# The router's gate on two fp32r parts of y and 32 columns, in place of three bf16 parts and 48

## The chip, the cores and the metric

One NeuronCore of a Trainium2 chip runs the whole program. The metric is the device time of one execution in microseconds. TensorE (PE; its weight loads are shown as PEld), VectorE (DVE), ScalarE (ACT) and GpSimd (POOL) run beside each other; SyncE (SP) issues most DMAs. Instructions of one engine start in the order in which they stand in its queue.

## The reference

Four batches of 2496 rows by 256 go through a spectral layer, and its output y is the input of a mixture of eight experts with the two best per row.

```python
X = np.fft.rfft(x, axis=1)
Yr = Xr @ w_r - Xi @ w_i + b_r            # and Yi; then soft thresholding with 0.01
y = np.fft.irfft(Yr + 1j * Yi, n=2496, axis=1)

logits = y @ w_gate                       # [9984, 8]
noise_scale = np.log1p(np.exp(y @ w_noise))
noisy_logits = logits + noise_scale * noise
top2 = np.argpartition(-noisy_logits, 2, axis=1)[:, :2]
...                                       # softmax over the two: top2_w
for each expert e, for each row that chose it:
    out += top2_w * (np.maximum(y @ w1[e], 0.0) @ w2[e])
```

The change is in the product of y with `w_gate` and `w_noise`, 16 columns together. Which experts a row chooses depends on it, so it is computed to nearly full float32 precision from parts.

## The kernel before

**Spectral stage.** Each batch is worked off in ten steps, c = 0 to 39 over the four batches. A step makes `z` (`mix`, the products with `w_r` and `w_i`), `y` (`s2`), and the first half of the inverse transform `u` (`is2`, sent to a scratch tensor `ud`). All of these multiply float32 values as fp32r parts: a high part, cast by ScalarE, and the rest, subtracted by VectorE. Between two batches stands stage 1 of the next one (`s1`, product `s`, plain float32).

**Last half and gate.** While batch b+1 goes through the spectral stage, batch b is finished in 11 tiles of up to 2 x 117 rows (the last has 2 x 78): `fin` makes the rows `f` and copies them to `yf`, `gate_a` transposes them on PE into `yt` and takes the first part, `gate_b` takes the others, `gate_c` multiplies them by the weights into `lg` and sums the parts with a reduction into `ls`. In these products the piece of y is the stationary operand (117 or 78 columns), the weights are the moving one. `route` then turns `ls` into choices, and `scatter` sends the rows to the region of their expert.

**What sets the order.** The steps of `fin`, gate (G), `route` (R) and `scatter` (S) are queued as closures, and two plans name the slot of the main loop at which each is called: `put` in the main loop for batches 0 to 2, two gate steps in each c, and `expert_plan` for batch 3, whose gate runs inside the first expert blocks. A step j of the gate before runs `gate_c(j-2)`, `gate_b(j-1)` and `gate_a(j)`; there are 13 of them per batch. Inside these limits the framework orders each engine's instructions by its own estimate of when their data are ready; only SP's are kept as written. Buffers of the pools are given in the code by `bufs`.

**Experts.** 40 blocks of 512 rows follow; each has 48 products `p` of 512 columns in the first layer (`blk_L1`, parts `hh` and `hl` behind it) and 64 in the second (`blk_L2`). The first block's first layer begins while the last batch leaves the spectral stage. I call this place the hand-over; there VectorE also works off `route` of batch 2, whose tiles are all called `rt`.

Of the kernel before, what the change touches and what calls it, by code (L numbers as in the profile page):

```python
# [43 lines left out]
def expert_plan(todo):  # L44

    mp = {(i, k): "" for i in range(12) for k in range(12)}

    def put(kind, n, i, k, every):
        if len(every) == 1:
            mp[i, k] += kind * n  # L50
            n = 0
        while n:
            if k in every:
                mp[i, k] += kind
                n -= 1
# [81 lines left out]
def tile_spectral_moe(ctx: ExitStack, tc: tile.TileContext, x, w_r, w_i, b_r, b_i, w_gate, w_noise,  # L137
# [77 lines left out]
    w3 = const.tile([128, 2, 48], BF16, name="w3", tag="w3")  # L215
# [32 lines left out]
    def late_loads():  # L248
        Es = tail.tile([117, 22, 39], F32, name="Es", tag="UT", bufs=4)
        last["es"] = Es  # L250
        nc.sync.dma_start(Es, c_inv)
        nc.sync.dma_start(wgn[:, :, 0:NE], w_gate.rearrange("(c p) d -> p c d", p=128))
        nc.sync.dma_start(wgn[:, :, NE:], w_noise.rearrange("(c p) d -> p c d", p=128))
        rest = wgn
        for k in range(3):
            nc.gpsimd.tensor_copy(w3[:, :, 16 * k:16 * k + 16], rest)
            if k < 2:
                nxt = const.tile([128, 2, 16], F32, name=f"wrest{k}", tag=f"wrest{k}")
                nc.gpsimd.tensor_sub(nxt, rest, w3[:, :, 16 * k:16 * k + 16])
                rest = nxt  # L260
        nc.sync.dma_start(nzt, noise)

    def expand_e(a):
# [143 lines left out]
    def np_(j):  # L407
        return PT if j < 10 else 78

    def gate_a(b, j):  # L410

        P, yf = np_(j), YF[b, j]
        yt = ps.tile([128, 2, 2, 128], F32, name=f"yt{b}_{j}", tag="B", bufs=NBK)
        for i in range(2):
            for dc in range(2):
                nc.tensor.transpose(yt[:, i, dc, :P], yf[:P, i, 128 * dc:128 * dc + 128], ident[:P, :P])  # L416
        y3 = tail.tile([128, 3, 2, 2, PT], BF16, name=f"y3{b}_{j}", tag="y3", bufs=2)
        r1 = tail.tile([128, 2, 2, PT], F32, name=f"r1{b}_{j}", tag="r1", bufs=1)
        YS[b, j] = (y3, r1)
        nc.scalar.copy(y3[:, 0, :, :, :P], yt[:, :, :, :P])  # L420
        nc.vector.tensor_sub(r1[:, :, :, :P], yt[:, :, :, :P], y3[:, 0, :, :, :P])

    def gate_b(b, j):
        P = np_(j)
        y3, r1 = YS[b, j]
        nc.scalar.copy(y3[:, 1, :, :, :P], r1[:, :, :, :P])
        nc.vector.tensor_sub(y3[:, 2, :, :, :P], r1[:, :, :, :P], y3[:, 1, :, :, :P])

    def gate_c(b, j):
        P = np_(j)  # L430
        y3, _ = YS.pop((b, j))
        if j == 0:
            LS[b] = tail.tile([PT, TT, 16], F32, name=f"ls{b}", tag="ls", bufs=1)
            nc.vector.memset(LS[b][:, 20:], 0.0)
        if j % 5 == 0:
            LG[b] = ps.tile([128, 10, 48], F32, name=f"lg{b}_{j}", tag="LG", bufs=1)
        for i in range(2):
            o = LG[b][:P, 2 * (j % 5) + i, :]
            for dc in range(2):
                for k in range(3):  # L440
                    nc.tensor.matmul(o, y3[:, k, i, dc, :P], w3[:, dc, :], start=dc == k == 0, stop=dc == 1 and k == 2)  # L441
        if j % 5 == 4 or j == 10:
            h, n = 10 * (j // 5), 10 if j < 10 else 2
            nc.vector.tensor_reduce(out=LS[b][:P, h:h + n], in_=LG[b][:P, :n].rearrange("p t (k c) -> p t c k", k=3),
                                    axis=AX.X, op=ALU.add)

    RT = {}
# [344 lines left out]

    def queue_gate(b):
        def step(j):
            if j >= 2:
                gate_c(b, j - 2)
            if 1 <= j < 12:
                gate_b(b, j - 1)
            if j < 11:
                gate_a(b, j)  # L800

        for j in range(13):
            todo["G"].append(lambda j=j: step(j))

    def queue_route(b):
# [57 lines left out]
    for b in range(NB - 1):  # L863
# [1 line left out]
        f = c + (2, 3, 4)[b]  # L865
        put("U", 1, f - 2, 0, ev)
        put("F", 11, f, 0, (0, 2, 4, 6, 8))
        p = put("G", 13, f, 3, (1, 3, 5, 7, 9))
# [67 lines left out]
    blk_L1(0, 0)  # L936
    ysplit(b, 8)
    s2(b, 9)
    do("G" * (len(todo["G"]) - 13))
    is2(b, 8)  # L940
    blk_L1(0, 1)
    ysplit(b, 9)
# [109 lines left out]
```

## Time and profile before

| | us |
|---|---|
| median of 3 timed runs (lowest, highest) | 1255.1 (1250.47, 1260.01) |
| the profiled execution, its own time | 1242.59 |
| its span, first to last instruction | 1240.9 |
| PE busy | 1214.5 |
| VectorE busy | 837.9 |
| ScalarE busy | 721.5 |
| POOL busy | 472.5 |

The span is what the trace covers; the execution's own time has 1.7 us around it. Busy times are unions of records. PE's records are pipelined: each shows its own latency, so a group's busy time is not its share of PE, and the pace of short matmuls is read from the distances between their starts. The gate of batches 0 to 2 runs from 99 to 317 us, that of batch 3 up to 437 us.

### The profile page before, as it was taken

How to read it: one execution, taken by the hardware profiler on the slowest of the kernel's cores; microseconds unless marked ns; L12 is line 12 of the kernel's file. 1: busy time of each engine (PE TensorE's matmuls, PEld its weight loads, DVE VectorE, ACT ScalarE, POOL GpSimd, SP SyncE). 2: the span in 40 equal slices, each digit the busy share in tenths (PEclk: the TensorE clock that was granted, in tenths of full speed). 3: DMA queues.
4: the chain of work that ended last, by engine and by line, in shares of the span. 5: the costliest groups of instructions: out<-in, count | busy, mean ns of one | idle time of the engine just before them, and what ended most of it. 6: DMA issues, size and time to landing. Idle time of an engine off the chain costs nothing.

```text
span 1240.9 us, 18977 instructions
## 1 busy us (share of the span) xinstructions
PE 1214.5 (98%) x6596; PEld 1030.0 (83%) x6596; DVE 837.9 (68%) x1709; ACT 721.5 (58%) x1367; POOL 472.5 (38%) x374
## 2 busy tenths in 40 slices
PE   7999999999899999999999999999999999999996
PEld 6888888888688888888888888888888888888885
DVE  4867887788866697566665666656566665666652
ACT  3656677778666676565555545555455554555542
POOL 3000035464345677877323232232322323233232
PEclk9999999999999999999999999999999999999998
DMA  6646645265758769996866656666565766657641
GB/s 173 184 146 215 220 125 185 92 210 135 234 120 195 178 157 248 251 248 166 179 132 149 158 140 146 124 152 154 145 149 118 151 154 146 153 118 147 152 98 24
DMA packets 224693, 197.68 MB, mean 159 GB/s; under 512 B 116967, under 2 KB 203901, under 8 KB 224590
## 3 DMA queue, kind: packets, MB, share of 16 engines
q1 hardware_dynamic: 190206, 153.18, 45.9%
q0 software_dynamic: 34384, 43.21, 18.7%
q8 instruction: 54, 0.88, 0.3%
q14 instruction: 49, 0.40, 0.1%
HBM read 107.46 MB, written 67.90 MB: 141 GB/s over the span
## 4 chain that ended last, share of the span: by engine, by line
PE 94%; DVE 2%; DMA 1%; ACT 1%; issue 0%; POOL 0%; SPq 0%; POOLq 0%; ACTq 0%; DVEq 0%
PE p L756 36%; PE p L739 34%; PE z L321 9%; PE y L334 4%; PE f L401 3%; PE u L365 2%; PE lg L441 2%; PE yt L416 1%; DMA wf<-w_i 1%; PE s L291 1%; DMA x<-x 0%; DVE hl L743 0%; ACT L474 0%; DVE rt L489 0%; DVE rt L493 0%
## 5 line engine op out<-in xcount | busy, mean ns | idle before, releaser
L762 POOL DMA_INDIRECT out<-ot,si x160 | 271.3, 1696 | 474.1 <-DVE f L683 344.5
L756 PE MATMUL p<-w2p,hh 128*128 128x512 f32 x1280 | 444.5, 395 | 0.1
L756 PE MATMUL p<-w2p,hl 128*128 128x256 f32 x1280 | 332.4, 280 | 0.7 <-DVE hl L743 0.7
L557 POOL DMA_INDIRECT xs_d<-yx,rt x176 | 190.4, 1082 | 271.8 <-ACT yx L552 210.5
L743 DVE SCALAR_TENSOR_TENSOR hl<-p,hh 128x512 fp32r<-128x512 f32 x320 | 220.1, 688 | 101.7 <-ACT hh L742 100.7
L742 ACT ACTIVATE hh<-p 128x512 fp32r<-128x512 f32 x320 | 191.6, 599 | 134.0 <-PE p L739 133.7
L756 PEld LDWEIGHTS p<-w2p,hh 128*128 128x128 f32 x1280 | 232.4, 188 | 44.1 <-DVE w2p L718 0.4
L739 PE MATMUL p<-xh,w1h 128*128 128x512 f32 x640 | 251.8, 393 | 3.8 <-DVE hl L743 3.8
L756 PEld LDWEIGHTS p<-w2p,hl 128*128 128x128 f32 x1280 | 241.0, 188 | 14.6 <-DVE hl L743 1.3
L739 PE MATMUL p<-xl,w1h 128*128 128x512 f32 x640 | 250.0, 391 | 0.0
L739 PE MATMUL p<-xh,w1l 128*128 128x512 f32 x640 | 249.6, 390 | 0.0
L760 ACT ACTIVATE o<-p,wt 128x256 f32<-128x256 f32 x160 | 75.9, 474 | 243.5 <-PE p L756 243.2
L761 DVE SCALAR_TENSOR_TENSOR ot<-p,wt,o 128x256 f32<-128x256 f32 x160 | 77.1, 482 | 187.3 <-ACT o L760 187.3
L739 PEld LDWEIGHTS p<-xh,w1h 128*128 128x128 f32 x640 | 120.5, 188 | 28.3 <-DVE hl L743 4.7
L739 PEld LDWEIGHTS p<-xh,w1l 128*128 128x128 f32 x640 | 120.6, 188 | 25.3
L739 PEld LDWEIGHTS p<-xl,w1h 128*128 128x128 f32 x640 | 120.6, 188 | 24.9
L718 DVE TENSOR_TENSOR w1l<-w1r,w1h 128x512 fp32r<-128x512 f32 x160 | 108.7, 685 | 15.6 <-ACT w1h L715 15.5
L715 ACT CAST w1h<-w1r 128x512 fp32r<-128x512 f32 x160 | 97.7, 618 | 17.9 <-PE p L739 17.9
L718 DVE TENSOR_TENSOR w2p<-w2r,w2p 128x512 fp32r<-128x512 f32 x160 | 103.8, 687 | 2.2 <-ACT w2p L715 1.2
L715 ACT CAST w2p<-w2r 128x512 fp32r<-128x512 f32 x160 | 91.0, 620 | 0.0
L321 PE MATMUL z<-wh,th 128*128 128x512 f32 x160 | 66.1, 413 | 2.0 <-ACT th L306 2.0
L324 DVE TENSOR_TENSOR zl<-z,zh 128x512 fp32r<-128x512 f32 x80 | 54.8, 687 | 17.4 <-ACT zh L323 16.6
(153 smaller groups left out, 1423.0 us busy)
## 6 DMA issues: line engine op xcount, KB each, us to landing
w1r<-w SPq DMA_DIRECT2D x40, 1024.0 KB
w2r<-w SPq DMA_DIRECT2D x40, 1024.0 KB
out<-zero SPq DMA_DIRECT2D x16, 656.0 KB
x<-x SPq DMA_DIRECT2D x20, 468.0 KB
UT<-ud SPq DMA_DIRECT2D x60, 156.0 KB
ud<-us SPq DMA_DIRECT2D x36, 256.0 KB
xs_d<-zero SPq DMA_DIRECT2D x9, 528.0 KB
xs_d<-yx,rt POOLq DMA_INDIRECT x176, 4.7
```

Source lines behind the costliest of these rows:

```text
L321: nc.tensor.matmul(z, t[:, dc, 128 * h:128 * h + 128], ww[:, dc, :], start=k == 0, stop=k == 5)
L324: nc.vector.tensor_sub(zl[:, h], z, zh[:, h].bitcast(F32))
L557: st = nc.gpsimd.indirect_dma_start(out=xs_d, out_offset=bass.IndirectOffsetOnAxis(ap=ix[:P, 2 * j + n, k:k + 1], axis=0), in_=yx[:P, n, : ...
L715: cp = nc.scalar.copy(h, r)
L718: nc.vector.tensor_sub(l, r, h.bitcast(F32))
L739: nc.tensor.matmul(p, a[:, dc, 128 * f:128 * f + 128], b[:, dc], start=k == 0, stop=k == 5)
L742: last["act"] = nc.scalar.activation(hh, p, AF.Relu).ins
L743: last["dve"] = nc.vector.scalar_tensor_tensor(out=hl, in0=p, scalar=0.0, in1=hh.bitcast(F32), op0=ALU.max, op1=ALU.subtract).ins
L756: nc.tensor.matmul(o, a[:, sl], b, start=f == n == 0, stop=f == 7 and n == 1)
L760: nc.scalar.activation(o1, p[:, 1], AF.Copy, scale=wt)
L761: nc.vector.scalar_tensor_tensor(out=ot, in0=p[:, 0], scalar=wt, in1=o1, op0=ALU.mult, op1=ALU.add)
L762: st = nc.gpsimd.indirect_dma_start(out=out, out_offset=bass.IndirectOffsetOnAxis(ap=si[:, m:m + 1], axis=0), in_=ot, in_offset=None, comp ...
```

## The change

`gate_a` now casts the transposed tile to an fp32r part `gh` and subtracts it from the tile into a second fp32r part `gl`. `gate_b` and its two operations are gone. The weights are two fp32r parts side by side, 32 columns, `w2g`. `gate_c` makes four products for each of the two halves of a tile (two parts by two chunks of 128 of the 256 columns of y), eight per tile in place of twelve; the reduction adds two groups of 16 columns in place of three. A step j of the gate runs `gate_c(j-1)` and `gate_a(j)`, 12 steps per batch, so routing is called one gate slot earlier.

```diff
-    p = put("G", 13, 1, 1, (1, 4, 7, 10))
+    p = put("G", 12, 1, 1, (1, 4, 7, 10))
...
-        rest = wgn
-        for k in range(3):
-            nc.gpsimd.tensor_copy(w3[:, :, 16 * k:16 * k + 16], rest)
-            if k < 2:
-                nxt = const.tile([128, 2, 16], F32, name=f"wrest{k}", tag=f"wrest{k}")
-                nc.gpsimd.tensor_sub(nxt, rest, w3[:, :, 16 * k:16 * k + 16])
-                rest = nxt
+        nc.gpsimd.tensor_copy(w2g[:, :, :16], wgn)
+        nc.gpsimd.tensor_sub(w2g[:, :, 16:], wgn, w2g[:, :, :16].bitcast(F32))
...
-        y3 = tail.tile([128, 3, 2, 2, PT], BF16, name=f"y3{b}_{j}", tag="y3", bufs=2)
-        r1 = tail.tile([128, 2, 2, PT], F32, name=f"r1{b}_{j}", tag="r1", bufs=1)
-        YS[b, j] = (y3, r1)
-        nc.scalar.copy(y3[:, 0, :, :, :P], yt[:, :, :, :P])
-        nc.vector.tensor_sub(r1[:, :, :, :P], yt[:, :, :, :P], y3[:, 0, :, :, :P])
-
-    def gate_b(b, j):
-        P = np_(j)
-        y3, r1 = YS[b, j]
-        nc.scalar.copy(y3[:, 1, :, :, :P], r1[:, :, :, :P])
-        nc.vector.tensor_sub(y3[:, 2, :, :, :P], r1[:, :, :, :P], y3[:, 1, :, :, :P])
+        gh, gl = YS[b, j] = [tail.tile([128, 2, 2, PT], F32R, name=f"g{n}{b}_{j}", tag=f"g{n}") for n in "hl"]
+        nc.scalar.copy(gh[:, :, :, :P], yt[:, :, :, :P])
+        nc.vector.tensor_sub(gl[:, :, :, :P], yt[:, :, :, :P], gh[:, :, :, :P].bitcast(F32))
...
-            LG[b] = ps.tile([128, 10, 48], F32, name=f"lg{b}_{j}", tag="LG", bufs=1)
+            LG[b] = ps.tile([128, 10, 32], F32, name=f"lg{b}_{j}", tag="LG", bufs=1)
         for i in range(2):
-            o = LG[b][:P, 2 * (j % 5) + i, :]
-            for dc in range(2):
-                for k in range(3):
-                    nc.tensor.matmul(o, y3[:, k, i, dc, :P], w3[:, dc, :], start=dc == k == 0, stop=dc == 1 and k == 2)
+            for n in range(4):
+                nc.tensor.matmul(LG[b][:P, 2 * (j % 5) + i, :], g2[n // 2][:, i, n % 2, :P], w2g[:, n % 2, :],
+                                 start=n == 0, stop=n == 3)
...
         def step(j):
-            if j >= 2:
-                gate_c(b, j - 2)
             if 1 <= j < 12:
-                gate_b(b, j - 1)
+                gate_c(b, j - 1)
             if j < 11:
                 gate_a(b, j)
```

The other two lines with 13 (the plan of batches 0 to 2, and the call of what is left before the hand-over) become 12 as well.

On PE, at the first tile of batch 0, the order was this (a matmul with bf16 operands has its load as a row of its own; `w` is the gate's weights):

```order
L416 MATMUL yt_0_960<-ident,yf_0_912 128x117 x4
L334 MATMUL y_2_1014<-zh_2_897,FG 128x512
L321 MATMUL z_4_0_1072<-wh,th_4_999 128x512
L321 MATMUL z_4_0_1072<-wl,th_4_999 128x512
L441 LDWEIGHTS y_0_965
L441 MATMUL lg_0_1045<-w_116,y_0_965 117x48
L321 MATMUL z_4_0_1072<-wh,tl_4_1000 128x512
L321 MATMUL z_4_0_1072<-wh,th_4_999 128x512
L321 MATMUL z_4_0_1072<-wl,th_4_999 128x512
L321 MATMUL z_4_0_1072<-wh,tl_4_1000 128x512
L401 MATMUL f_2_986<-UT_1_834,E 117x256 x2
L416 MATMUL yt_1_1005<-ident,yf_1_942 128x117 x4
```

It is now this:

```order
L411 MATMUL yt_0_955<-ident,yf_0_907 128x117 x4
L329 MATMUL y_2_1018<-zh_2_892,FG 128x512
L316 MATMUL z_4_0_1067<-wh,th_4_994 128x512
L316 MATMUL z_4_0_1067<-wl,th_4_994 128x512
L426 MATMUL lg_0_1000<-w2g,gh_0_960 117x32 x2
L316 MATMUL z_4_0_1067<-wh,tl_4_995 128x512
L316 MATMUL z_4_0_1067<-wh,th_4_994 128x512
L316 MATMUL z_4_0_1067<-wl,th_4_994 128x512
L316 MATMUL z_4_0_1067<-wh,tl_4_995 128x512
L396 MATMUL f_2_981<-UT_1_829,E 117x256 x2
L426 MATMUL lg_0_1000<-w2g,gl_0_961 117x32 x2
L426 MATMUL lg_0_1000<-w2g,gh_0_960 117x32 x2
```

All eight products of the first tile now stand ahead of the second tile's transposes, where one of twelve did.

On PE at the hand-over, the last gate tile of batch 2 (`lg_10`) stood among the first expert block's products:

```order
L365 MATMUL u_8_3841<-yh_8_3790,FG 128x512
L365 MATMUL u_8_3841<-yl_8_3791,FG 128x512
L365 MATMUL u_8_3841<-yh_8_3790,FG 128x512
L739 MATMUL p_1_3848<-xh_3773,w1h_3287 128x512
L739 MATMUL p_1_3848<-xl_3774,w1h_3287 128x512
L739 MATMUL p_1_3848<-xh_3773,w1l_3288 128x512
L739 MATMUL p_1_3848<-xh_3773,w1h_3287 128x512
L441 LDWEIGHTS y_10_3740
L441 MATMUL lg_10_3827<-w_116,y_10_3740 78x48
```

Now:

```order
L426 MATMUL lg_10_3628<-w2g,gh_10_3556 78x32 x2
L426 MATMUL lg_10_3628<-w2g,gl_10_3557 78x32 x2
L426 MATMUL lg_10_3628<-w2g,gh_10_3556 78x32 x2
L426 MATMUL lg_10_3628<-w2g,gl_10_3557 78x32 x2
L360 MATMUL u_8_3638<-yh_8_3606,FG 128x512
L360 MATMUL u_8_3638<-yl_8_3607,FG 128x512
L360 MATMUL u_8_3638<-yh_8_3606,FG 128x512
L725 MATMUL p_1_3645<-xh_3589,w1h_3150 128x512
```

The tile's products have moved ahead of `u_8` and `p_1`.

On VectorE at the same place, before, from the last tile's reduction on (`hl` is the second part behind the experts' first layer, `c`, `yl` belong to the spectral stage):

```order
L444 TENSOR_REDUCE ls_3261<-lg_10_3827 78x32
L743 SCALAR_TENSOR_TENSOR hl_1_3856<-p_1_3848,hh_1_3855 128x512
L470 SCALAR_TENSOR_TENSOR rt_4_3904<-ls_3261 117x176
L356 TENSOR_TENSOR yl_9_3860<-c_9_3808,yh_9_3859 128x512
L473 TENSOR_SCALAR rt_2_3902<-rt_1_3901 117x176
L477 SCALAR_TENSOR_TENSOR rt_4_3904<-rt_2_3902,rt_1_3901 117x176
L478 TENSOR_TENSOR rt_3_3903<-rt_3_3903,rt_4_3904 117x176
```

Now:

```order
L430 TENSOR_REDUCE ls_3086<-lg_10_3628 78x32
L342 TENSOR_SCALAR c_9_3624<-t_9_3623 128x512
L456 SCALAR_TENSOR_TENSOR rt_4_3701<-ls_3086 117x176
L343 TENSOR_TENSOR c_9_3624<-t_9_3623,c_9_3624 128x512
L459 TENSOR_SCALAR rt_2_3699<-rt_1_3698 117x176
L463 SCALAR_TENSOR_TENSOR rt_4_3701<-rt_2_3699,rt_1_3698 117x176
L351 TENSOR_TENSOR yl_9_3657<-c_9_3624,yh_9_3656 128x512
L729 SCALAR_TENSOR_TENSOR hl_1_3653<-p_1_3645,hh_1_3652 128x512
L464 TENSOR_TENSOR rt_3_3700<-rt_3_3700,rt_4_3701 117x176
```

The reduction and the first of the routing now stand ahead of `c_9`, and `hl_1` has moved behind the routing's first three operations and `yl_9`.

## Rows read from the trace of the kernel before

**Rows 1.** The page, parts 1 and 4: busy times, and the chain that ended last.

```profile
PE 1214.5 (98%) x6596; PEld 1030.0 (83%) x6596; DVE 837.9 (68%) x1709; ACT 721.5 (58%) x1367; POOL 472.5 (38%) x374
...
PE 94%; DVE 2%; DMA 1%; ACT 1%; issue 0%; POOL 0%; SPq 0%; POOLq 0%; ACTq 0%; DVEq 0%
PE p L756 36%; PE p L739 34%; PE z L321 9%; PE y L334 4%; PE f L401 3%; PE u L365 2%; PE lg L441 2%; PE yt L416 1%; DMA wf<-w_i 1%; PE s L291 1%; DMA x<-x 0%; DVE hl L743 0%; ACT L474 0%; DVE rt L489 0%; DVE rt L493 0%
```

**Rows 2.** Busy times by stretch: length, PE, PEld, DVE, ACT, POOL, clock, DMA.

```profile
99.00:145.00 46.00, 46.00 (x326) 38.42 (x326) 36.28 (x63) 30.90 (x57) 0.00 (x0) 1.00 0.69 221
...
310.00:331.00 21.00, 17.22 (x102) 13.92 (x101) 17.19 (x42) 12.67 (x23) 6.32 (x6) 0.92 0.64 190
```

**Rows 3.** Waits of PE: total us, times, longest.

```profile
PE lg L441 <- DVE y L427: 0.4, 1, 0.4
PE yt L416 <- DVE r L421: 0.4, 1, 0.4
```

**Rows 4.** Groups by line and shape: busy us, mean ns, idle before.

```profile
L441 PE MATMUL lg<-w,y 128*117 128x48 bf16 x480 | 33.0, 210 | 0.6 <-DVE y L427 0.4
L427 DVE TENSOR_TENSOR y<-r,y 128x468 bf16<-128x468 f32 x40 | 25.7, 643 | 7.9 <-ACT y L426 7.6
L426 ACT CAST y<-r 128x468 bf16<-128x468 f32 x40 | 23.5, 588 | 13.8 <-DVE r L421 13.8
L441 PE MATMUL lg<-w,y 128*78 128x48 bf16 x48 | 2.6, 194 | 0.0
```

**Rows 5.** Timeline of PE at 107 us: start, us, instruction.

```profile
107.55 0.78 PE L441 MATMUL lg<-w,y 128*117 128x48 bf16 x12
```

**Rows 6.** Timeline of PE at 316 us, the hand-over.

```profile
315.82 0.48 PE L739 MATMUL p<-xl,w1h 128*128 128x512 f32 x1
316.14 0.39 PE L739 MATMUL p<-xh,w1l 128*128 128x512 f32 x1
316.37 0.53 PE L441 MATMUL lg<-w,y 128*78 128x48 bf16 x10
317.94 0.50 PE L739 MATMUL p<-xh,w1h 128*128 128x512 f32 x1 [1.05 <-DVE hl L743]
```

**Rows 7.** Timeline of PE, stage 1 of batches 1 and 2.

```profile
78.76 0.72 PE L291 MATMUL s<-C,x 78*128 78x80 f32 x5
...
158.15 2.82 PE L291 MATMUL s<-C,x 117*128 117x120 f32 x24
```

**Rows 8.** Records by line: min/median/max ns, first and last start, forms.

```profile
L291 PEld LDWEIGHTS s<-C,x x352: 186/192/338, 6.1 to 240.6; 117*128 117x128 f32 x160, 78*128 78x128 f32 x16
L291 PE MATMUL s<-C,x x352: 242/275/537, 6.1 to 240.7; 117*128 117x120 f32 x160, 78*128 78x80 f32 x16
...
L756 PEld LDWEIGHTS p<-w2p,hl x1280: 186/188/208, 331.8 to 1229.3; 128*128 128x128 f32 x183
...
L441 PEld LDWEIGHTS <-y x528: 113/134/136, 100.3 to 436.8; 128*117 128x117 bf16 x160, 128*78 128x78 bf16 x16
...
L416 PEld LDWEIGHTS yt<-ident,yf x176: 137/141/168, 99.0 to 421.7; 117*128 117x128 f32 x160, 78*128 78x128 f32 x16
...
L401 PE MATMUL f<-UT,E x176: 377/378/475, 96.3 to 408.9; 117*117 117x256 f32 x160, 78*78 78x256 f32 x16
```

**Rows 9.** Timeline of PE at 602 us, the experts' second layer.

```profile
601.75 0.28 PE L756 MATMUL p<-w2p,hl 128*128 128x256 f32 x1
601.86 0.39 PE L756 MATMUL p<-w2p,hh 128*128 128x512 f32 x1
```

**Rows 10.** Timeline at the hand-over, VectorE's routing and PE's long wait.

```profile
317.80 0.33 DVE L470 SCALAR_TENSOR_TENSOR rt<-ls 117x176 f32<-117x176 f32 x1
...
325.14 0.17 DVE L501 TENSOR_TENSOR rt<-rt,rt 117x22 f32<-117x22 f32 x1
...
325.97 0.80 PE L739 MATMUL p<-xh,w1h 128*128 128x512 f32 x1 [2.74 <-DVE hl L743]
```

**Rows 11.** Busy times by stretch, right behind that wait.

```profile
326.00:329.00 3.00, 3.00 (x7) 2.44 (x8) 2.31 (x4) 0.07 (x1) 0.00 (x0) 0.50 0.80 227
```

More of the change, by code (lines that the diff above doesn't have):

```diff
@@ L214, in tile_spectral_moe @@
     wgn = const.tile([128, 2, 16], F32, name="wgn", tag="wgn")
-    w3 = const.tile([128, 2, 48], BF16, name="w3", tag="w3")
+    w2g = const.tile([128, 2, 32], F32R, name="w2g", tag="w2g")
     nzt = const.tile([PT, NB * TT, NE], F32, name="nzt", tag="nzt")
@@ L416, in gate_a @@
                 nc.tensor.transpose(yt[:, i, dc, :P], yf[:P, i, 128 * dc:128 * dc + 128], ident[:P, :P])
-        y3 = tail.tile([128, 3, 2, 2, PT], BF16, name=f"y3{b}_{j}", tag="y3", bufs=2)
-        r1 = tail.tile([128, 2, 2, PT], F32, name=f"r1{b}_{j}", tag="r1", bufs=1)
-        YS[b, j] = (y3, r1)
-        nc.scalar.copy(y3[:, 0, :, :, :P], yt[:, :, :, :P])
-        nc.vector.tensor_sub(r1[:, :, :, :P], yt[:, :, :, :P], y3[:, 0, :, :, :P])
-    def gate_b(b, j):
-        P = np_(j)
-        y3, r1 = YS[b, j]
-        nc.scalar.copy(y3[:, 1, :, :, :P], r1[:, :, :, :P])
-        nc.vector.tensor_sub(y3[:, 2, :, :, :P], r1[:, :, :, :P], y3[:, 1, :, :, :P])
+        gh, gl = YS[b, j] = [tail.tile([128, 2, 2, PT], F32R, name=f"g{n}{b}_{j}", tag=f"g{n}") for n in "hl"]
+        nc.scalar.copy(gh[:, :, :, :P], yt[:, :, :, :P])
+        nc.vector.tensor_sub(gl[:, :, :, :P], yt[:, :, :, :P], gh[:, :, :, :P].bitcast(F32))
     def gate_c(b, j):
         P = np_(j)
-        y3, _ = YS.pop((b, j))
+        g2 = YS.pop((b, j))
         if j == 0:
@@ L435, in gate_c @@
         if j % 5 == 0:
-            LG[b] = ps.tile([128, 10, 48], F32, name=f"lg{b}_{j}", tag="LG", bufs=1)
+            LG[b] = ps.tile([128, 10, 32], F32, name=f"lg{b}_{j}", tag="LG", bufs=1)
         for i in range(2):
-            o = LG[b][:P, 2 * (j % 5) + i, :]
-            for dc in range(2):
-                for k in range(3):
-                    nc.tensor.matmul(o, y3[:, k, i, dc, :P], w3[:, dc, :], start=dc == k == 0, stop=dc == 1 and k == 2)
+            for n in range(4):
+                nc.tensor.matmul(LG[b][:P, 2 * (j % 5) + i, :], g2[n // 2][:, i, n % 2, :P], w2g[:, n % 2, :],
+                                 start=n == 0, stop=n == 3)
         if j % 5 == 4 or j == 10:
             h, n = 10 * (j // 5), 10 if j < 10 else 2
-            nc.vector.tensor_reduce(out=LS[b][:P, h:h + n], in_=LG[b][:P, :n].rearrange("p t (k c) -> p t c k", k=3),
+            nc.vector.tensor_reduce(out=LS[b][:P, h:h + n], in_=LG[b][:P, :n].rearrange("p t (k c) -> p t c k", k=2),
                                     axis=AX.X, op=ALU.add)
@@ L794, in step @@
         def step(j):
-            if j >= 2:
-                gate_c(b, j - 2)
             if 1 <= j < 12:
-                gate_b(b, j - 1)
+                gate_c(b, j - 1)
             if j < 11:
                 gate_a(b, j)
-        for j in range(13):
+        for j in range(12):
             todo["G"].append(lambda j=j: step(j))
@@ L867, in tile_spectral_moe @@
         put("F", 11, f, 0, (0, 2, 4, 6, 8))
-        p = put("G", 13, f, 3, (1, 3, 5, 7, 9))
+        p = put("G", 12, f, 3, (1, 3, 5, 7, 9))
         two = [k for k in (5, 7, 9) if (c + 9, k) > p]
@@ L938, in tile_spectral_moe @@
     s2(b, 9)
-    do("G" * (len(todo["G"]) - 13))
+    do("G" * (len(todo["G"]) - 12))
     is2(b, 8)
```

## The prediction

> **What bounds the kernel now.** I read the page first: PE is busy for 1214.5 of 1240.9 us, and the chain that ended last runs over PE for 94% of the span, with 2% on the gate's product `lg` and 1% on its transposes `yt` [rows 1]. So a nanosecond more or less on PE is one in the time, unless PE waits there. Next the stages: the gate works between 99 and 437 us, and in the three stretches where it shares PE with the spectral batches PE's records leave no gap at all, 46.00 us of 46.00 in the first of them and the same in the other two [rows 2]. PE's waits there are small: 0.4 us for `y` and 0.4 us for `r` in all [rows 3]. The exception is 310 to 331 us, where the spectral stage hands over to the experts: PE is busy 17.22 of 21 us at a mean clock of 0.92 [rows 2]. VectorE and ScalarE have room in every stretch. So I cost the change on PE first, then look at that hand-over, then at what the lighter vector work is worth.
>
> **The gate's matmuls, the main term.** Before there are 528 of them, 480 on full tiles and 48 on the short last tile of a batch [rows 4]. A record of a matmul shows a latency of some 0.2 us; the pace is the distance from start to start. Twelve on a full tile take 0.78 us with the last one's own 0.21 in it, so (0.78-0.21)/11 = 0.052 us each [rows 4, 5]; ten on the short tile take 0.53, (0.53-0.19)/9 = 0.038 us [rows 4, 6]. The pace goes with the 117 or 78 columns of the stationary operand, the piece of y; the moving 48 columns are the same in both. So each matmul is paced by its weight load, and 32 moving columns in place of 48 save nothing. What counts is the number of loads, 528 to 352, and what one costs.
>
> After the change the loaded piece is 4 bytes wide. How such a load paces a short matmul is not shown for fp32r. Plain f32 shows it: 24 of stage 1's records take 2.82 us, (2.82-0.24)/23 = 0.112 us each; of these, 16 have 120 moving columns and 8 have 80, and five of the 80-column kind alone are no quicker, (0.72-0.24)/4 = 0.12 [rows 7, 8]. So that pace is the load of 128 columns. The load records say that fp32r behaves likewise: 188 ns for 128 columns of fp32r (`hh`), 192 for 128 of plain f32 (`x`), but 134 for 117 and 113 for 78 of bf16, and 141 for 128 columns in the transposes [rows 8]. The 47 ns between 188 and 141 are about one more pass over 128 columns (my estimate from the 21 ns between 117 and 78 columns, 0.54 ns each, is 69). And a 512-column matmul that comes behind gate matmuls starts its successor 0.32 us later, at 315.82 and 316.14, where the usual distance is 0.23 [rows 6]: about 0.09 us of its own fp32r load stays uncovered behind a short matmul. Against it stands that fp32r loads fit under a 256-column matmul, whose step of 0.11 us (601.75 to 601.86) leaves room for either [rows 9]. I take 0.112 x 117/128 = 0.102 us for a full tile and 0.068 for the short one. Bounds: 0.052 and 0.038 if fp32r loads like bf16, 0.112 for both if columns don't matter.
>
> The first matmul of a run has its load under the wide matmul ahead, and the last one pays for the load of what follows, so the pace counts inside runs only. Counted in the order, gate matmuls stand in 54 runs before and 49 after: 431 steps on full tiles and 43 on short ones before, 275 and 28 after. Before: 431 x 0.052 + 43 x 0.038 = 24.0 us. After: 275 x 0.102 + 28 x 0.068 = 30.0 us. Five runs fewer save five exits of about 0.12 us, -0.6. **Sum on PE: +5.4 us**; by the bounds 275 x 0.052 + 28 x 0.038 = 15.4, so -9.2, or 303 x 0.112 = 33.9, so +9.3.
>
> **Vector work.** Removed: the second cast of each tile, 23.5 us on ScalarE for the full ones, and the second subtraction, 25.7 us on VectorE [rows 4]. The first pair stays, with another output type. The reduction reads a third less. All this is worth nothing where PE has no gap [rows 2]; the most it could return is PE's two waits for the gate, 0.8 us [rows 3]. I count 0. Were PE to wait there, a cast and a subtraction would each be worth their 0.6 us per tile.
>
> **A gate step earlier.** The matmuls of a tile now come one step after its transposes, not two, so the cast and the subtraction must be done within that step. A pair takes some 0.59+0.64 us [rows 4] plus queues. In the order nearly every step leaves eleven or more wide matmuls of 0.23 us, over 2.5 us of PE work, in between; two tiles at the start of batch 3, inside an expert block, leave about 1.5. There I expect 1 us of waiting, where there is about 0.8 now [rows 3]. Behind such a wait PE's next products queue. +0 to +1.5; I take +0.3.
>
> **The hand-over.** Here PE waits 1.05 us at 317.94 and 2.74 us at 325.97, where a record takes 0.80 us in place of 0.39 [rows 6, 9, 10]: after PE's pause the granted clock is 0.50 of full speed, 1.2 GHz, for 3 us [rows 11]. What ends the long wait is `hl` on VectorE, which stands behind the routing chain of batch 2, from 317.80 to 325.14 [rows 10]. That chain starts at the reduction of the last gate tile. With one gate step fewer that tile's matmuls come ahead of `u_8` and `p_1`, so the reduction starts some nine wide matmuls (9 x 0.23 = 2.1 us) earlier on PE's scale; but the new order puts `hl_1` behind the exponential and `yl_9`, and the logarithm's table load of ScalarE behind `hh_1`. Going through the new rows with the old durations I get the second wait ending about 0.9 us earlier relative to `p_1`, with the 0.4 us of ten late gate matmuls moved ahead: **-1 us**, between -4.2 (wait and slow clock both gone: 2.74, and half of the 3 us at half speed) and +2.
>
> POOL loses three operations of 32 columns near the program's start; POOL has 0% of the chain [rows 1], so 0 us. No DMA moves across another on SP's queue.
>
> **Sum**: +5.4 + 0.3 - 1 = +4.7 us on a profiled execution of 1242.6 us (span 1240.9). That execution lies 1% below the median of the timed runs, 1255.1; the same +4.7 there gives **1260 us**, +0.4%.
>
> **Rivals.**
> *A: a load costs by columns whatever its type.* Then the gate gives 9.2 us back, and with -1 + 0.3 the time is 1255.1 - 9.9 = 1245.2 us, -0.8%. For it: nothing here shows an fp32r load pacing a short matmul directly. Against it: 188 against 141 ns, and 0.32 against 0.23 us [rows 6, 8].
> The Trainium skill speaks for A and so against my sum: "TensorE: Matmul & The Clock Gate", section LDWEIGHTS, gives a load's time as its columns over 1.2 GHz and names no type. By its figure, an estimate, 117 columns are 0.0975 us for both kinds, and the gate would save some 17 us (about 1238 us); the trace's bf16 pace of 0.052 disagrees with that figure [rows 5].
>
> *B, slower: a narrow fp32r matmul is run like a plain f32 one*, as two records. The product `f` shows the split: 88 matmuls, 176 records [rows 8]. The price is 320 x 0.102 + 32 x 0.068 = 34.8 us more, 1295 us, +3.2%. It decides if there is a width of the moving operand, between 256 and 32 columns, below which fp32r is split. Against it: `hl` with 256 columns shows 1280 loads for its 40 x 4 x 8 = 1280 matmuls [rows 8].
> The Trainium skill, "FP8 and Floating Point Precision", section TensorE Precision Notes, gives four passes to true FP32 and describes reduced precision as one truncated read, with no width in it; for the widths seen here, the trace agrees.
>
> *C: the hand-over gets worse*: `hl_1` now waits behind the exponential, a second pause of the 2.74 us kind with its slow clock, +4.2 in place of -1: 1265 us.
>
> **Chances.** Forecast 0.74 (1255 to 1266), A 0.14, B 0.05, C 0.07. The low end takes in A; the high end the bound +9.3 with +2. The runs before spread from 1250 to 1260, so a median may lie a few us off either way: range 1243 to 1268. 1% is about what a measurement of this kernel can tell from no change. A alone lands at -0.8%, and a third of it beyond 1%: 0.05 faster. B and a little of the rest: 0.07 slower. Within 1%: 0.88.
>
> **What would show it.** Timeline of PE: runs of eight gate matmuls at a pace near 0.10 us (A: 0.05; B: 16 records). Load records of the gate near 175 ns, not 134. Counts of 352 records. Busy times without `r` and the third part of y. In the hand-over: a wait for `hl` near 2 to 3 us, followed by long records. PE still without gaps from 99 to 310 us; gaps of over 0.3 us at the gate's matmuls there would show that the shorter distance between transposes and matmuls was too short, and would make me wrong upward. A pace of 0.05 would make me wrong downward.

## The result and the profile after

The changed kernel takes 1268.21 us (median of 6 runs, 1262.38 to 1275.98). Before takes 1254.12 us beside it (6 runs, 1249.66 to 1260.01). The ratio is 1.0107, with a 95% interval of 1.0085 to 1.0129: slower by 1.1%, where the forecast was 1260.0 us, +0.4%. 1268.21 lies just above the upper end of the range, 1268.

The two pages must not be subtracted from each other. The execution of before that was profiled took 1242.6 us, that of after 1267.2, and 24.6 us is more than the 14 us by which the medians differ. Before comes in two levels here: in some sets of runs its median was 1241 to 1242 us, in others 1254 to 1256, and each kernel below is compared with before in its own set. The profile of before belongs to the first level, that of after to the second. I call them the 1241 level and the 1255 level. The sets of e5 to e8 and of e9 to e12 were measured on one and the same chip, the first at the 1241 level and the second at the 1255 level, so the chip alone doesn't set it.

First the load records of the gate's products, from the groups of after (busy us and mean ns of one behind the bar), the answer to [rows 8]:

```profile
L426 PEld LDWEIGHTS lg<-w2g,gh 128*117 128x117 f32 (+1 forms) x176 | 27.5, 179 | 6.5 <-issue 2.0 <-ACT gh L413 1.0
L426 PEld LDWEIGHTS lg<-w2g,gl 128*117 128x117 f32 (+1 forms) x176 | 25.4, 182 | 0.9 <-DVE gl L414 0.4
```

352 loads, and 179 to 182 ns each where the bf16 loads took 134. Then the eight products of one tile in PE's timeline of after (start, us, instruction), the answer to [rows 5]:

```profile
106.45 0.28 PE L426 MATMUL lg<-w2g,gh 128*117 128x32 f32 x2
106.58 0.36 PE L426 MATMUL lg<-w2g,gl 128*117 128x32 f32 x2
106.79 0.36 PE L426 MATMUL lg<-w2g,gh 128*117 128x32 f32 x2
106.99 0.36 PE L426 MATMUL lg<-w2g,gl 128*117 128x32 f32 x2
107.20 0.52 PE L411 MATMUL yt<-ident,yf 117*128 117x117 f32 x3
```

From 106.58 to 106.99 four products pass, 0.41 us, so 0.102 us each. The prediction said 0.102. On the short tile the distance from start to start is 0.070 us, where it said 0.068. There are eight records for eight matmuls, so nothing is split in two.

The stretches of after (length, PE, PEld, DVE, ACT, POOL, clock, DMA), the answer to [rows 2]:

```profile
99.00:145.00 46.00, 45.99 (x273) 38.88 (x273) 29.95 (x53) 25.16 (x46) 0.00 (x0) 1.00 0.64 208
225.00:262.00 37.00, 33.50 (x201) 29.75 (x201) 26.94 (x78) 23.47 (x45) 15.62 (x16) 0.91 0.27 78
262.00:310.00 48.00, 44.58 (x228) 36.35 (x227) 34.17 (x68) 30.39 (x57) 24.92 (x25) 0.96 0.66 184
310.00:331.00 21.00, 21.00 (x132) 18.29 (x131) 15.33 (x31) 13.20 (x25) 7.84 (x8) 1.00 0.37 114
```

The first stretch has no gap, as forecast. The next two have 3.5 and 3.4 us of them and a lower clock. They are the end of batch 1's gate, its routing and its scatters, which the prediction hadn't priced. The three stretches in which the prediction found no gap left out two of before, 145 to 180 and 225 to 262 us, in which the routing of batches 0 and 1 ends:

```profile
145.00:180.00 35.00, 34.36 (x201) 29.23 (x201) 30.83 (x91) 24.70 (x47) 4.59 (x4) 1.00 0.35 110
225.00:262.00 37.00, 36.67 (x232) 31.41 (x230) 32.54 (x100) 27.69 (x53) 20.24 (x20) 1.00 0.43 136
```

So "without gaps from 99 to 310 us" was not quite what before showed: PE stood for 0.6 and 0.3 us there, almost all of it before the product `pr` explained below. What ends PE's waits in all of after (total us, times, longest), the answer to [rows 3]:

```profile
...
PE pr L496 <- DVE rt L491: 4.5, 3, 2.9
PE p L742 <- DVE ot L747: 2.5, 2, 2.0
PE p L725 <- DVE hl L729: 2.3, 1, 2.3
...
PE u L360 <- ACT yf L397: 1.4, 1, 1.4
PE u L360 <- ACT yh L350: 1.0, 1, 1.0
...
PE lg L426 <- ACT gh L413: 0.6, 1, 0.6
```

The waits that the prediction looked at are there and small: 0.6 us for `gh`, 2.3 us in one piece at the hand-over, where [rows 6, 10] had 1.05 and 2.74. The large one is `pr`, the routing's rank product (the product of the choices `rt` with `ones` and `tri`, which counts how many tokens stand ahead of each): 2.9 us at batch 1, where before's profile, of the other level, has 0.33, and 1.25 us at batch 0, where it has 0.60.

### The profile page after: what moved, and what is told of

Same layout as the page of the kernel before. It is cut to its first block, busy times and chain, and to the rows that moved or that the text cites. A ratio compares the mean times of both kernels' runs of the same rounds, so it can differ in the third digit from the quotient of the medians.

```text
span 1265.4 us, 18516 instructions
## 1 busy us (share of the span) xinstructions
PE 1229.2 (97%) x6420; PEld 1043.0 (82%) x6420; DVE 816.2 (65%) x1665; ACT 703.5 (56%) x1323; POOL 466.3 (37%) x371
## 4 chain that ended last, share of the span: by engine, by line
PE 87%; issue 4%; POOL 3%; ACT 2%; DMA 2%; DVE 1%; another core or an unknown queue 0%; SPq 0%; POOLq 0%; ACTq 0%; DVEq 0%
PE p L742 35%; PE p L725 34%; PE z L316 6%; PE y L329 3%; POOL xs_d L543 3%; PE f L396 2%; PE lg L426 2%; PE u L360 2%; PE yt L411 1%; PE s L286 1%; DMA wf<-w_i 1%; DMA xs_d<-yx,rt 1%; ACT yx L537 0%; DMA x<-x 0%
## 5 line engine op out<-in xcount | busy, mean ns | idle before, releaser
L543 POOL DMA_INDIRECT xs_d<-yx,rt x176 | 185.6, 1055 | 296.7 <-ACT yx L538 244.0
```

The source lines that it names most:

```text
L543: st = nc.gpsimd.indirect_dma_start(out=xs_d, out_offset=bass.IndirectOffsetOnAxis(ap=ix[:P, 2 * j + n, k:k + 1], axis=0), in_=yx[:P, n, : ...
```

## The experiments

All edits are made to the changed kernel unless the text says before. The level of each set is named, since one part of the answer depends on it. All kernels compute all of the reference except e3, e7 and e17: these have y and the gate's weights in two bf16 parts, so fewer bits of both reach the gate.

### Loads and order, one at a time (1241 level)

e1 has the new parts in the old thirteen steps, with the products two steps behind the transposes:

```diff
-            if 1 <= j < 12:
-                gate_c(b, j - 1)
+            if j >= 2:
+                gate_c(b, j - 2)
-        for j in range(12):
+        for j in range(13):
-        p = put("G", 12, f, 3, (1, 3, 5, 7, 9))
+        p = put("G", 13, f, 3, (1, 3, 5, 7, 9))
```

> The fp32r parts of the change, with the gate's products two steps behind the transposes and 13 steps, as before the change; routing stands in its old slots, and the rank product of batch 1 behind the last piece of stage 1 again. Theory O (the step that is left out puts routing and its product one slot earlier on PE, whose wait there brings the slow clock): the loads still cost 5 to 6 us, the waits are those of before, so 1.004 to 1.005 times before. Theory P (all of it is the pace of the loads and what hangs on PE being later): as the changed kernel, 1.010 to 1.012.

Measured: 1249.43 against 1241.17 us, 1.0057 (1.0042 to 1.0071).

e2 is before with its three bf16 parts in the new order: twelve steps, the second cast and subtraction in the step of the first.

```diff
-            if j >= 2:
-                gate_c(b, j - 2)
-                gate_b(b, j - 1)
+                gate_c(b, j - 1)
+                gate_b(b, j)
```

> The three bf16 parts and 48 columns of before, all three taken in the step of the transposes, the products one step behind, 12 steps: the order of the change with the arithmetic of before. Theory O: 8 to 9 us more than before, 1.006 to 1.008, with PE waiting over 2 us at the rank product of batch 1 and 0.5 of the clock behind it. Theory P: 1.000 within 0.002.

Measured: 1246.88 us, 1.0053 (1.0038 to 1.0068), a little under what was expected of theory O. The wait of 2 us that theory O put at batch 1's rank product isn't there (0.04 us). The trace, of the fastest of the six runs (1245.37 us), shows 1.2 us at batch 0's (before 0.6) and 4.3 us at the hand-over (before 3.8).

e3 keeps the new order and the eight products, with two bf16 parts:

```diff
-    w2g = const.tile([128, 2, 32], F32R, name="w2g", tag="w2g")
+    w2g = const.tile([128, 2, 32], BF16, name="w2g", tag="w2g")
```

> The changed kernel with both parts of y and both of the weights in bf16 (the gate's product then carries fewer bits of y and of the weights, some choices of experts may differ): eight products per tile at the load pace of bf16, the order of the change. If the load of the 4-byte type is what the gate pays for, its products run at 0.05 us in place of 0.10, and 275 x 0.050 + 28 x 0.032 = 14.6 us go: 0.999 of before under theory O too, 0.996 under P, where the order costs nothing.

Measured: 1237.54 us, 0.9968 (0.9955 to 0.9980).

e4 keeps the new parts and the short distance of one step; an empty thirteenth gate step puts only what comes behind the gate, the routing and the scatters, back in its old places:

```diff
-        for j in range(12):
+        for j in range(13):
```

(and 13 for 12 where the planner places the steps, as in e1).

> The changed kernel with an empty 13th gate step, so that only routing and scattering return to their old slots; the gate's products stay one step behind. Theory O: as e1, 1.004 to 1.005. If instead the short distance between transposes and products makes PE wait: as the changed kernel, 1.010 to 1.012, and above e1. Theory P: 1.010 to 1.012.

Measured: 1249.26 us, 1.0064 (1.0049 to 1.0078). e1 and e4 differ only in the distance between transposes and products, and agree within their intervals. So the shorter distance costs nothing that can be measured, which by the intervals means less than some 2 us. e2 says that the order alone costs half a per cent with the old operands.

### Does the sum hold, and what is in it (1241 level)

> The changed kernel itself, beside the others. Sum theory: what the slower gate loads cost with the routing in its old place (e4: 1.0064, e1: 1.0057) and what the earlier routing costs with the old gate operands (e2: 1.0053) add up, so 1.011 of before, +13.5 us (1.009 to 1.013), and the trace has both marks: the half clock for some 6.8 us at 245, behind a wait for batch 1's rank product, and that for 6.8 us at batch 3's first gate tiles. Rival, the two hide in each other (both are idle or slow time of the matrix engine in the same stretches): 1.007, +8.5 us.

e5 is the changed kernel. Measured: 1249.84 against 1241.0 us, 1.0066 (1.0051 to 1.0080). The rival had it: at this level the order costs nothing on top of the new loads, and the sum theory that I had taken from e1 to e4 fell. e5 also isn't the 1.0107 of the first set.

> The changed kernel with the routing of batch 3 alone back in its old place (one empty gate step behind its twelve), that of batches 0 to 2 one slot earlier as in the changed kernel. If the order in the main loop costs the 0.5% (batch 1's rank product ahead of the last piece of stage 1, and the transfers and scatters behind it): as the changed kernel, 1.010 to 1.011, with the wait and the half clock at 245 still there. Rival, it is the hand-over behind batch 3, where my prediction put the whole cost of the earlier routing: 1.006, as with all four in their old places.

e8 has batch 3's routing alone in its old place (`range(13 if b == NB - 1 else 12)`). Measured: 1250.15 us, 1.0076 (1.0060 to 1.0093). With e4 and e5 as close as they are, this says nothing of the batches. Nor does it test the hand-over, as its expectation has it: the routing that runs there is batch 2's, and batch 3's rank product comes at 459 us, 131 us behind the hand-over's wait.

> Both parts of y and of the gate's weights in bf16 (two parts, so fewer bits of y and of the weights reach the gate's products than the reference keeps), eight products of 117 columns per tile where before had twelve, and the routing in its old place. Sum theory: e3 with the same operands and the earlier routing had 0.9968; without the earlier routing's 0.0050 this gives 0.992, -10 us, below both kernels. Rival, with fewer products the earlier routing costs nothing (the vector engine and the transfers are late either way): 0.9965, as e3.

e7 is e3 with the routing in its old place. Measured: 1235.05 us, 0.9944 (0.9929 to 0.9960). Against e3, of another set, the order costs 0.0024 here, and the two intervals touch. The distance from e4, which has the same products with fp32r operands, is 14.2 us (1249.26-1235.05, two sets of one level). By the paces it should be 275 x 0.050 + 28 x 0.030 = 14.6. PE's timeline of e7:

```profile
103.72 0.26 PE L426 MATMUL lg<-w2g,gh 128*117 128x32 bf16 x2
103.83 0.26 PE L426 MATMUL lg<-w2g,gl 128*117 128x32 bf16 x2
103.94 0.50 PE L411 MATMUL yt<-ident,yf 117*128 117x117 f32 x3
```

Four products in 0.22 us, 0.055 each by rows rounded to 0.01, with 32 moving columns. [rows 5] had 0.052 with 48. So 32 moving columns are no quicker than 48, as the prediction said, and the loaded type is what doubles the pace.

### The table of two by two (1255 level)

e9 is the changed kernel, e10 that of e4, e11 that of e2.

> The changed kernel once more, beside the three below: with before, e10 and e11 it makes a table of two by two on one chip, old and new order of the routing by old and new operands of the gate. Theory S (what the earlier routing costs stands for itself): 1.010 to 1.011, e10's 1.006 and e11's 1.005 together. Theory H (the earlier routing's waits are only long where transfers or the vector engine are late; where they are punctual they cost nothing beside the longer loads): 1.0066, as e5 had, and e10's ratio within 0.001 of it. Either way the runs' mean clock is 0.002 to 0.003 below that of before, which is 2.5 to 3.5 us of the difference.

> The changed operands with the routing in its old place (the kernel of e4). Both theories: 1.006, +7.5 us: +5.4 us for the loads, about +1.6 us for expert blocks that are 46.6 ns longer, and about +1 us for a lower clock. If the longer loads alone were the whole cost, as my prediction had it: 1.0044, +5.4 us.

> The old operands with the earlier routing (the kernel of e2). Theory S: 1.005, +6.5 us, as before. Theory H: the 1.0053 of e2 came from waits that change from run to run, so anything from 1.001 to 1.006, and with the mean clock of the runs: where that is 0.996, within 3 us of before. The expert blocks' pace is that of before either way.

Before took 1255.12 us in this set. Measured: e9 1267.85 us, 1.0109 (1.0075 to 1.0143); e10 1260.90 us, 1.0037 (1.0016 to 1.0058); e11 1260.91 us, 1.0047 (1.0027 to 1.0066). At this level theory S holds: 0.0037 + 0.0047 = 0.0084, inside the interval of e9, and the first result came back. The mean clock of the runs of e9 is 0.9885 and that of before 0.9918, a difference of 0.0033 where 0.002 to 0.003 was expected.

### Which batch (1255 level)

e14 gives batch 1 alone its old place:

```diff
-        for j in range(12):
+        for j in range(13 if b == 1 else 12):
-        p = put("G", 12, f, 3, (1, 3, 5, 7, 9))
+        p = put("G", 13 if b == 1 else 12, f, 3, (1, 3, 5, 7, 9))
```

> The changed kernel, for e14 and e15 beside it. Where before takes about 1255 us: 1.011 (1.008 to 1.014), with a wait of 2.8 us for batch 1's rank product near 246 and waits of 2 to 4 us between 270 and 290. Where before takes about 1241 us: 1.0066 (1.005 to 1.008), without these waits.

> The changed kernel with the routing of batch 1 alone in its old place (one empty gate step behind its twelve); batches 0, 2 and 3 as changed. If batch 1's earlier routing carries the cost (its rank product ahead of stage 1's last piece at 246, its scatters beside the loads and stores at 263 to 290): as e15, 1.004 to 1.006, and the waits between 270 and 290 gone. Rival, the cost is spread over the batches or lies at the hand-over behind batch 3: between e13 and e15 or as e13, 1.008 to 1.011. Where e13 and e15 lie within 0.002 of each other it tells nothing.

> All four batches' routing in the old place, changed operands (the kernel of e4 and e10): 1.0037 to 1.0064, the two values that it had; blocks 46.6 ns longer than before's.

Before took 1255.72 us. Measured: e13, the changed kernel, 1270.52 us, 1.0120 (1.0087 to 1.0152); e14 1259.41 us, 1.0046 (1.0022 to 1.0069); e15, all four batches in the old place, 1259.29 us, 1.0036 (1.0019 to 1.0053). One batch carries the cost: batch 1. The routing of batch 2, at the hand-over where the prediction looked, and that of batches 0 and 3 keep the new order in e14, which lies 0.001 above e15, less than the intervals. e14 moves the whole routing of batch 1 and the scatters behind it, so which of these costs what is read from traces alone.

PE's timeline of e13 and then of e15 shows the place (a bracket is the idle time before the row and its releaser):

```profile
244.90 0.93 PE L286 MATMUL s<-C,x 117*128 117x120 f32 x6 [0.44 <-issue]
248.78 0.47 PE L496 MATMUL pr<-rt,ones 117*128 117x176 bf16 x1 [2.95 <-DVE rt L491]
249.07 0.49 PE L497 MATMUL pr<-rt,tri 117*128 117x176 bf16 x1
249.38 1.81 PE L286 MATMUL s<-C,x 78*128 78x80 f32 x8
```

```profile
242.66 1.91 PE L286 MATMUL s<-C,x 117*128 117x120 f32 x16 [0.93 <-issue]
246.55 0.47 PE L496 MATMUL pr<-rt,ones 117*128 117x176 bf16 x1 [1.98 <-DVE rt L491]
246.84 0.49 PE L497 MATMUL pr<-rt,tri 117*128 117x176 bf16 x1
```

With the routing a slot earlier, `pr` of batch 1 stands ahead of the eight records of stage 1's last piece (the row with 78x80), which could have run in the wait. Behind them it waits 1.98 us, ahead of them 2.95; eight at 0.12 us [rows 7] are the 0.97 between. In the other traces of this level the wait is 2.8 to 3.0 us in the new order (after, e9, e11) and 1.9 to 2.1 in the old (e10, e12, e14, e16). At the 1241 level it is 0.1 us in e5, which has the new order too.

Why the product comes late at the 1255 level is seen on VectorE, in e13 and then in e5:

```profile
247.53 0.18 DVE L498 TENSOR_SCALAR rt<-rt 117x22 f32<-117x22 f32 x1 [4.46 <-ACT rt L488]
...
248.38 0.34 DVE L491 TENSOR_TENSOR rt<-rt,real 117x176 bf16<-117x176 f32 x1
```

```profile
243.29 0.38 DVE L498 TENSOR_SCALAR rt<-rt 117x22 f32<-117x22 f32 x1 [0.41 <-ACT rt L488]
```

L491 makes the choices that `pr` multiplies. By the code it doesn't need the exponential of L488, but L498, which does, stands ahead of it in VectorE's queue. On ScalarE the exponential stands among the copies of stage 1's product, and between 240 and 294 us these wait 6.2 us in e13 and 1.5 us in e5. In all nine traces of the 1255 level VectorE waits 3.3 to 4.5 us at this place, in those of the 1241 level 0.4 us or less, in either order of the routing. What holds the copies up isn't shown, and a queue with L498 behind L491 wasn't tried.

The rest of it comes behind that wait. The stretches of e13, e15 and e5, in this order:

```profile
225.00:262.00 37.00, 33.31 (x206) 29.54 (x205) 25.45 (x71) 23.61 (x46) 15.70 (x15) 0.91 0.24 74
262.00:294.00 32.00, 28.50 (x133) 22.35 (x132) 23.22 (x54) 18.01 (x34) 18.38 (x19) 0.96 0.65 198
```

```profile
225.00:262.00 37.00, 34.09 (x207) 29.91 (x205) 27.64 (x77) 23.53 (x45) 16.57 (x17) 0.95 0.29 88
262.00:294.00 32.00, 30.18 (x156) 24.70 (x155) 24.35 (x56) 21.60 (x43) 17.96 (x18) 1.00 0.73 205
```

```profile
225.00:262.00 37.00, 36.88 (x233) 31.97 (x232) 31.37 (x92) 26.53 (x51) 20.20 (x20) 1.00 0.35 116
262.00:294.00 32.00, 32.00 (x170) 26.72 (x170) 25.04 (x46) 24.40 (x46) 18.11 (x18) 1.00 0.76 208
```

In 69 us PE of e13 is idle for 3.69 + 3.50 = 7.2 us and loses 37 x 0.09 + 32 x 0.04 = 4.6 us to the clock, 11.8 together; 0.7 of it is counted twice, since the granted clock is 0.75 in the 2.95 us of the wait itself. e15 is idle for 2.91 + 1.82 = 4.7 us and loses 1.9 to the clock, 6.6 together. So 4.5 to 5.2 us lie here. The same sum for e9 and e10 gives 11.2 and 4.8 us, a difference of 6.4. The medians differ by 11.2 us (e13, e15) and 7.0 us (e9, e10): between two fifths and nine tenths of it is in these 69 us. For e14 the sum is 6.3 us, near e15's, though its profiled run is the slowest of its twelve (1266.99). In e5 the same stretches cost 0.1 us.

The idle time in the second stretch has this behind it, from ScalarE's waits in e13 between 240 and 294 us:

```profile
ACT us L366 <- PE z L316: 4.0, 1, 4.0
ACT yf L397 <- remote: 3.7, 1, 3.7
```

ScalarE stands 4.0 us before it may copy `u` into `us`, and 3.7 us before it may copy `f` into `yf`; behind them PE's `u` wait for `yh` and `yf` 1.1 and 1.4 us. The releaser of the first had long been done and the second has no name in the trace, so a transfer is likely for both, and which one stays open. e15 has 2.8 us at `us` too, and 3.7 us at `yf` in two pieces that end with PE's `f`; there PE's `u` waits 1.8 us for `yh` and not for `yf`. So this link is argued and not shown.

### Where the tiles lie

In every kernel with the new weights and no unused tile, an expert block that runs alone takes longer on PE than in before, though its 112 products are the same and none of them waits. Two starts ten blocks apart, in before and then in after:

```profile
568.21 0.39 PE L739 MATMUL p<-xh,w1h 128*128 128x512 f32 x1
...
788.74 0.39 PE L739 MATMUL p<-xh,w1h 128*128 128x512 f32 x1
```

```profile
591.15 0.39 PE L725 MATMUL p<-xh,w1h 128*128 128x512 f32 x1
...
812.15 0.39 PE L725 MATMUL p<-xh,w1h 128*128 128x512 f32 x1
```

220.53 and 221.00 us: 47 ns per block, some 1.6 us over the 35 blocks that run alone. e2 and e11, with the old weights, have 0. The new weights take 192 bytes per partition less among the constants, which moves the tiles that are laid from the left end of the memory, and the gate's new parts move those laid from the right end by 32 bytes (by the tile sizes in the code, each rounded up to 32 bytes; the traces hold no addresses). e6 gives the 192 bytes back with an unused tile:

```diff
+    const.tile([128, 48], F32, name="pad", tag="pad")
```

> The changed kernel with an unused tile of 192 bytes per partition behind the gate's new weights, so that every later tile lies at the address that it had before the change; nothing else differs. Placement theory: the 46.6 ns that each expert block takes longer in all kernels with the smaller pool of constants go away, 35 blocks, -1.6 us, so 0.0013 less than the changed kernel in the same rounds (1.0097 if that is 1.011). Rival, the 46.6 ns come with what the kernel computes or from the order and not from the place: the same ratio as the changed kernel, and the blocks still 46.6 ns longer.

Measured (1241 level): 1252.78 us (4 runs), 1.0096 (1.0080 to 1.0113), slower than e5, and 126.6 ns per block. The expectation was wrong twice: the pad doesn't put every tile back, since those on the right stay 32 bytes off, and the blocks got longer. But an unused tile had changed the time, so the place matters. e12 puts an unused tile of 64 bytes (`[128, 16]`) into before:

> The kernel before with one unused tile of 64 bytes per partition behind the gate's weights; no instruction differs, only the addresses of the tiles that come later. Placement theory (the expert blocks' pace hangs on where their tiles lie): blocks longer or shorter than before's by some 40 ns or more, as the 46.6 ns of the changed kernel and the 126.6 ns of e6, so a ratio of 0.999 to 1.003. Rival, the block's pace comes from something else that the change moves: 0 ns to within 2 ns, and 1.000.

Measured (1255 level): 1263.93 us, 1.0064 (1.0041 to 1.0087), from a tile that nothing reads or writes. Two starts ten blocks apart in e12:

```profile
583.31 0.39 PE L740 MATMUL p<-xh,w1h 128*128 128x512 f32 x1
...
804.91 0.39 PE L740 MATMUL p<-xh,w1h 128*128 128x512 f32 x1
```

221.60 us, 107 ns per block more than before, 3.7 us or 0.003 over 35 blocks. The other 0.003 (0.001 by the interval's lower end) isn't explained. e16 is e15 with an unused tile of 160 bytes, so that both sides lie 32 bytes below their places in before:

> e15 with an unused tile of 160 bytes per partition behind the gate's new weights: the tiles on the left side of the memory then lie 32 bytes below their places in before, as those on the right side do in all fp32r kernels, so the distances between the two sides are those of before. If the blocks' pace hangs on the distance: 0 ns against before's blocks in place of 46.6, -1.6 us, 0.0013 below e15. If it hangs on each side's own address: 20 to 130 ns longer or shorter, 0.9995 to 1.003 of e15. If it doesn't hang on the place: 46.6 ns, as e15.

Measured, in the set of e13 to e15: 1257.63 us, 1.0025 (1.0005 to 1.0046).

```profile
583.34 0.39 PE L726 MATMUL p<-xh,w1h 128*128 128x512 f32 x1
...
803.87 0.39 PE L726 MATMUL p<-xh,w1h 128*128 128x512 f32 x1
```

220.53 us, the pace of before to the nanosecond, and 0.0011 below e15, whose interval overlaps. e17 tests the same rule where both sides move by 3680 bytes:

> The kernel of e7 (y and the gate's weights as two bf16 parts, routing in its old place) with an unused tile of 4000 bytes per partition behind the gate's weights: both sides of the memory then lie 3680 bytes above their places in before, at before's distance from each other. Distance theory: the blocks' pace is before's to within 1 ns (e7 had 46.6 ns more), and the ratio 0.992 to 0.9945, below e7's 0.9944 by 0.0013. Rival, e16's 0 ns was a chance of its addresses: 20 to 130 ns per block, 0.9945 to 0.998.

Measured (1241 level): 1234.54 against 1241.84 us, 0.9939 (0.9923 to 0.9955), 0 ns per block, which is the test. The ratio is 0.0005 below e7's, where 0.0013 was expected; the intervals allow either. It is the quickest kernel of the study, below both before and after, by the paces of the loads and not by the fp32r parts.

## Why the prediction was wrong

**The gate's matmuls: right, in mechanism and in size.** The pace is that of the load, 0.102 and 0.070 us, the moving columns are free, 352 records stand for 352 matmuls. Rivals A and B fall with these rows. e7 against e4, 14.2 us where the paces give 14.6, is the price of the wider type by itself. The Trainium skill, "TensorE: Matmul & The Clock Gate", section Weight-path perf modes, says that a quicker load takes two bf16 elements at a time and gives nothing for fp32, and that it needs 128 columns. Two to one is what the trace shows, but with 117 and 78 columns; there the measurement decides.

**Vector work: not separated.** PE's waits for the gate's cast and subtraction are 0.6 us and less each in after, 1.2 us in all where before had 0.9, so nothing was returned at the gate. At the hand-over the lighter work may have returned 1.5 us (below); no run changes it alone.

**A gate step earlier: the step that failed.** The text priced one effect of it, the shorter distance from a tile's transposes to its products, at +0.3 us. e1 and e4 show that this effect is 0 within some 2 us. But the same twelve steps also move everything that is queued behind the gate, the routing and the scatters of all four batches, one slot earlier. I followed that at the hand-over alone, where batch 2's routing runs, and took "no gap on PE" in three stretches of before's profile as a reason that it costs nothing elsewhere; the stretches with the rank products of batches 0 and 1 were not among them. At the 1255 level it costs 0.0072 (e9 less e10) to 0.0084 (e13 less e15), 9 to 10.5 us, nearly all of it at batch 1 (e14). The rank product of that batch passes stage 1's last piece, PE waits for VectorE with work behind it in the queue, and the clock falls; that the copies of `us` and `yf` wait because of it is argued. At batch 0 the earlier routing has PE wait 1.2 us at either level (e5, e9, e13), where e4, e10 and e15 have 0.1; e14 keeps this wait and lies 0.001 above e15.

**The hand-over: near in size, by luck.** After has 2.3 us of waiting there, in one piece, where [rows 6, 10] have 3.8 in two: 1.5 us less, where the text took 1. But its reason, the step that is left out, isn't the one. All kernels with fp32r parts and the short distance have 2.3 us, with the routing in its old place (e4, e10, e15) as in the new, at either level; e1, with the old steps, has 2.5. The old parts in the new order (e2 and e11) have more than before:

```profile
PE p L739 <- DVE hl L743: 4.3, 2, 3.3
```

So the new parts shorten this wait and the earlier routing doesn't; whether by the lighter work of VectorE or by something else that the parts change isn't separated. And since e5 and e4, e13 and e15 have the same wait here, the hand-over isn't the cause of the loss. Rival C had the nearest time, 1265 us, from the wrong place: a pause of PE with a low clock behind it, but at batch 1 and not at the hand-over.

**The sum.** Taken without the order and with the tiles in their old distance (e16) the change costs 0.0025 (0.0005 to 0.0046), and the forecast of 0.0039 lies inside; so would a sum of 1 us or of 5.5. The place of the tiles adds 0.0013 by the blocks' pace (0.0011 between e15 and e16, whose intervals overlap), the earlier routing the rest, up to 1.0107 to 1.0120.

**The range.** Its base was the median of three runs, 1255.1, which held (1254.12), but the waits were read from a profile 12.5 us quicker (1242.6). At that level (e5) the change costs 1.0066, 8.8 us where the sum said 4.7, and the earlier routing nothing that can be told from 0. The sum lacks two terms that the traces show. One is the longer blocks, 1.6 us. The other is the clock behind batch 3's first gate tiles. PE's waits there are small, as forecast (1.2 us, before 0.9), but in e5 the granted clock is at half speed for 6.8 us behind them: its mean from 345 to 365 us is 0.83, in before 1.00, which is worth 3.4 us. The same 6.8 us at half speed stand there in after, e1, e4, e10, e13, e14 and e15, half of them in e3, e6 to e8, e11, e16 and e17, none in e2, e9 and e12; e1 has the old distance, so the distance isn't what brings them. By these numbers 5.4 + 1.6 + 3.4 - 1.5 at the hand-over is 8.9 us, an estimate that no run tests term by term.

What stays open: what makes before take 1241 us in some sets and 1255 in others. The traces of the 1255 level show PE idle for 0.6 to 1.4 us in stage 1 between 240 and 251 us, waiting for nothing that the profile shows, beside the late copies of ScalarE behind which the routing falls back; those of the 1241 level don't. Also open is why the order alone costs 0.0053 at the 1241 level with three bf16 parts (e2), 0.0024 with two (e7 and e3) and 0.0002 with fp32r parts (e5 and e4).

## What to carry to other kernels

When a step of a queue is dropped, price every place at which the work behind it moves up, in each batch, and above all where an operation that waits for a slow chain passes work that could have filled the wait. "No gap" in one profile is not slack: look at the runs' own spread, and ask what waits would appear in an execution that is 1% longer. The gate's short matmuls are paced by the load of their stationary operand, so its type and columns count and 32 or 48 moving columns don't; whether it pays to make y the moving operand was not tried. Look in each queue for an operation that stands ahead of a critical one without being needed by it, as L498 does here.

## What the runs showed of the hardware that I had not expected

The pace of matmuls that never wait hangs on where their tiles lie. The distance between the tiles laid from the left and those laid from the right, against that of before, and the longer block: 0 bytes, 0 ns (e16 and e17, at -32 and +3680 bytes from before's places); +32 bytes, 126.6 ns (e6); +64, 106.6 (e12); -160, 46.6 (after, e1, e4); -4000, 46.6 (e3, e7). The two distances with 46.6 ns lie 3840 bytes apart, which would fit a pattern that repeats, but one pair doesn't show it. Two kernels were built to keep the distance and both came out at 0, so the distance is shown to matter; what it does inside the memory is not. A tile of 64 bytes that nothing touches made a kernel 0.6% slower, half of it by the pace of its blocks.

A pause of 2 to 3 us on PE is paid twice. Between 225 and 262 us e13 has 3.7 us of idle time and the granted clock at 0.91, which is 3.3 us more (0.7 of it inside the wait); e5 has 0.1 us and 1.00. In all nine traces of the 1255 level a stretch of 3.4 or 6.8 us at half speed begins in the wait for batch 1's `pr`, 1.9 to 3.0 us long, or up to 1 us behind it.
